# Agent attention and an ELU feed-forward layer on one core: half rounds of 512 query tokens with a tail of 192, one GpSimd pass of low parts a step, two of eight steps in float32

## The chip, the core and the metric

The kernel runs on one core of a Trainium2 chip. TensorE (PE) multiplies matrices; VectorE (DVE), ScalarE (ACT) and GpSimd (POOL) do the elementwise work; the SyncE queue (SP) issues the DMAs. The metric is the device time of one execution in microseconds, lower is better.

## The reference

Two batches of 12480 tokens with 128 channels go through attention by way of 49 agents, and the result through a feed-forward layer of width 2048 with ELU. Queries, keys and agents are drawn with a standard deviation of 0.8, so that the softmaxes are not flat.

```
def sm(a, b):
    s = scale * (a @ b.transpose(0, 2, 1))
    s = s - s.max(-1, keepdims=True)
    e = np.exp(s)
    return e / (e.sum(-1, keepdims=True) + 1e-09)
agent_v = sm(agents, k) @ v
x = sm(q, agents) @ agent_v                      # (2, 12480, 128)
h = x @ w_in                                      # 128 -> 2048
g = np.where(h > 0, h, np.exp(np.minimum(h, 0)) - 1)
out = g @ w_out                                   # 2048 -> 128
```

All inputs and the output are float32; the weights w_in and w_out are float64 and are converted on the chip.

## The kernel before

Since q2a @ agent_v @ w_in is associative, the kernel makes A = agent_v @ w_in once a batch (49 agents by 2048, `A_pe`, `A_out`) and never forms x. The probabilities of the queries, transposed to agents by tokens, are the moving operand of a first product with A, which gives h; the ELU of h is the moving operand of a second product with w_out.

*Tiles.* A round is G = 960 query tokens, 8 tiles (R) of 120 (TP), 13 rounds (NG) a batch, 26 in all. A tile's 120 tokens stand on partitions 0 to 59 and 64 to 123 (TQ = 124, HP = 60). A half round is T = 480 tokens, and a step is one half round with one of NP = 8 chunks of 256 hidden units: S = 416 steps. A step's tiles are 128 partitions by 2 x 480.

*A step.* `p1` (L418) multiplies: A and the probabilities are each split into a high part in float32r and the rest, also in float32r, and three products (high by high, high by low, low by high) are summed, each as a pair of matmuls on the upper and the lower half of the array's rows (`ROWS` = 0 and 64, tiles px and py, of which py is a copy of px with the halves exchanged, made by DMA, L355 and L356). `elu` takes exp(h - 1) on ACT (L424, bias from the tile `mone`) and min(e, 1) max h on DVE (L426), which is ELU + 1; the surplus is taken off at the end through the column sums of w_out (`w_sums`, `ncs`). `split` casts this g to a high part (float32r, ACT, L205) and subtracts it for the low part (`rest`, L210), in two passes of 480 columns: the first on POOL, the second on POOL or, in the chunks of `LO_DVE` = 0, 2 and 7, on DVE. `p2` (L456) sums low w by high g, high w by high g, high w by low g: six pairs of matmuls. In the one chunk of `PLAIN` = 3 there is no split; w and g are multiplied in float32, four matmuls, which the trace records as eight. After chunk 7 the two PSUM halves are joined: a DVE copy (L468), an ACT pass with `ncs` (L471), a POOL sum (L472) and the output DMA.

*Order.* The schedule is written by hand. The loop over steps at the end of the kernel issues in step s: `p1(s)`, `p2(s - 4)` (LAG), `elu(s)`, `split(s - 1)`, then what `at(s, ...)` has put there. A visit (`visit`, `plan`) is the attention work of one PSUM slot: scores of queries (L297) or of the second batch's keys (L166), or its sum of values (L225). After a query visit come, at fixed steps, the exponential, the sum (L317), the guard of 1e-9 and the reciprocal (`q_rz`: L322 and L325), the normalisation into `pp` (`q_mul`, L331), and the ring (`q_ring`): transposes on PE (L337), px on ACT and DVE, four DMAs to py. PSUM has three slots of two banks for h and visits (`ps_h`) and one bank each for the two output sums (`ps_o`).

*Prologue.* Scores of the first batch's keys (`sc`) alternate with the conversion of the weights (`conv`: `f64_steps`, L105 to L118, on DVE, ACT and POOL, with scratch tiles fr and ex in two buffers each; the product on POOL goes to `win_sb`, or for w_out to a passing tile "even", from which w_hi and w_lo are made); then come the exponentials, the sum over the values (L225), `w_sums` (L488) and A for the first batch.

Of the kernel before, what the change touches and what calls it, by code (L numbers as in the profile page):

```python
# [16 lines left out]
TP = 120  # L17
HP = TP // 2
TQ = 64 + HP
# [5 lines left out]
def tile_agent_attention_moe(  # L25
# [19 lines left out]
    T = G // 2  # L45
    NG = N // G
    NR = NG
    S = B * NG * NM
# [26 lines left out]
    w_f = big.tile([128, len(PLAIN), 2, 128], F32)  # L75
# [22 lines left out]
    def f64_steps(raw, out):  # L98
# [3 lines left out]
        fr = conv_pool[0].tile([128, n], I32, tag="fr", name="fr")  # L102
        ex = conv_pool[0].tile([128, n], I32, tag="ex", name="ex")
# [23 lines left out]

    def load_q(j):
        b, r = divmod(j, NG)
        t = kq_p.tile([C, G], F32, tag="q", name="q", bufs=2)  # L130
        nc.sync.dma_start(out=t, in_=qT[b, :, r * G:(r + 1) * G])
        q_t[j] = t
# [157 lines left out]
    def q_scores(j, ps):  # L290
        q_st[j] = {"ps": ps}
        src = q_t.pop(j)
        for t in range(R):
            for u in range(0, TQ, groups[0]):
                w = min(groups[0], TQ - u)
                x = t * TP + u - (64 - HP) * (u >= 64)
                nc.tensor.matmul(out=ps[u:u + w, t * NA:(t + 1) * NA], lhsT=src[:, x:x + w], rhs=ag_sb[:, j // NG, :], start=True, stop=True)  # L297

    def q_max(j):
        v = q_st[j]["ps"][:TQ, 0:R * NA].rearrange("p (t a) -> p t a", a=NA)  # L300
        mx = sm_p.tile([TQ, R], F32, tag="mx", name="mx")
        nc.vector.tensor_reduce(out=mx, in_=v, axis=AX.X, op=ALU.max)  # L302
        q_st[j]["mx"] = mx

    def q_sub(j):
        ps = q_st[j].pop("ps")
        v = ps[:TQ, 0:R * NA].rearrange("p (t a) -> p t a", a=NA)
        e = sm_p.tile([TQ, R, NA], F32, tag="qe", name="qe", bufs=2)
        nc.vector.tensor_tensor(out=e, in0=v, in1=q_st[j]["mx"].unsqueeze(2).to_broadcast([TQ, R, NA]), op=ALU.subtract)
# [17 lines left out]
    def q_mul(j):
        e = q_st[j]["e"].rearrange("p (h i) a -> p h i a", h=2)
        z = q_st[j]["z"].rearrange("p (h i) -> p h i", h=2).unsqueeze(3).to_broadcast([TQ, 2, R // 2, NA])
        out = pp.rearrange("p i (h a) -> p h i a", h=2)[:, :, :, 0:NA]  # L330
        nc.vector.tensor_tensor(out=out, in0=e, in1=z, op=ALU.mult)  # L331

    def q_tr(j, ps):
        for i in range(R // 2):
# [3 lines left out]
        q_st[j]["tr"] = ps[:NA2, :, 0:T // 2].rearrange("p u (i t) -> p u i t", t=HP)  # L338
# [4 lines left out]
    def q_parts(j, part):  # L343
# [3 lines left out]
        x = sm_p.tile([NA2, T], F32R, tag=f"px{part}", name=f"px{part}")  # L347
        y = sm_p.tile([NA2, T], F32R, tag=f"py{part}", name=f"py{part}")
# [6 lines left out]
        nc.sync.dma_start(out=y[a].bitcast(F32), in_=x[b].bitcast(F32))  # L355
# [448 lines left out]
```

## Time and profile before

| | us |
|---|---|
| median of 3 runs | 971.9 (971.7 to 974.7) |
| the profiled execution | 973.33 |
| its span, first to last instruction | 971.6 |
| PE busy | 949.6 (98%) |
| weight loads on PE busy | 796.2 (82%) |
| ACT busy | 847.6 (87%) |
| POOL busy | 833.8 (86%) |
| DVE busy | 807.5 (83%) |

The main loop of steps begins at about 58.6 us, with the first matmul of L418, and its last matmul starts at 966.9 us. The mean granted clock of TensorE is 0.994 of full speed. Durations in the rows are those of this one execution; a matmul's end is modelled, so the spacing of starts says more than a duration.

### The profile page before, as it was taken

Reading aid. Unit: us, or ns where it says so; the run is one execution under the profiler, and the core shown is the slowest. Engines: PE = TensorE matmul, PEld = TensorE weight load, DVE = VectorE, ACT = ScalarE, POOL = GpSimd, SP = SyncE. Lnnn points to the kernel's source line nnn. Section 1 sums busy time; section 2 is a strip of 40 time slices with the busy share of each in tenths; the row PEclk is TensorE's granted clock in tenths of the full one; section 3 lists DMA queues with packets and bytes.
Section 4 is the critical chain, followed back from the end, with each engine's and each line's share of the span. In section 5 each row is a group of like instructions: output and inputs, shape, how many; then the busy total and the mean of one; then the engine's idle time right before and its main releaser. Section 6 shows DMA issues by size and latency. Waiting matters only on the chain.

```text
span 971.6 us, 26490 instructions
## 1 busy us (share of the span) xinstructions
PE 949.6 (98%) x10894; PEld 796.2 (82%) x10894; DVE 807.5 (83%) x948; ACT 847.6 (87%) x967; POOL 833.8 (86%) x648
## 2 busy tenths in 40 slices
PE   7889999999999999999999999999999999999997
PEld 5777888888888888887888889788888888798886
DVE  7849788889888888788888889888988888898876
ACT  4648999988989889988998998989989989989996
POOL 3237888888988988988998998998989989989997
PEclk9989999999999999999999999999999999999999
DMA  9941232224232211012002101111020021001000
GB/s 349 398 141 53 99 94 78 68 74 119 68 93 79 68 32 58 28 42 68 27 26 64 37 27 52 38 39 59 20 79 27 22 68 38 27 12 37 28 21 21
DMA packets 26195, 67.47 MB, mean 69 GB/s; under 512 B 3239, under 2 KB 15171, under 8 KB 26075
## 3 DMA queue, kind: packets, MB, share of 16 engines
q1 hardware_dynamic: 26075, 65.79, 20.4%
q8 instruction: 85, 1.39, 0.6%
q14 instruction: 35, 0.29, 0.1%
HBM read 43.11 MB, written 12.78 MB: 58 GB/s over the span
## 4 chain that ended last, share of the span: by engine, by line
PE 79%; DVE 11%; issue 4%; ACT 3%; POOL 1%; DMA 1%; SPq 0%; POOLq 0%; DVEq 0%; ACTq 0%
PE o L456 49%; PE h L418 24%; DVE g L426 4%; PE h L225 3%; DVE lo L210 2%; ACT e L424 2%; POOL lo L210 1%; PE h L297 1%; PE h L166 1%; DVE ob L468 1%; DVE pp L331 1%; ACT hi L205 1%; DVE m_all L174 1%; DMA k<-in_kT_dram 1%; DVE mx L302 1%
## 5 line engine op out<-in xcount | busy, mean ns | idle before, releaser
L210 POOL TENSOR_TENSOR lo<-g,hi 128x480 fp32r<-128x480 f32 x571 | 744.3, 1339 | 96.6 <-ACT hi L205 37.4
L426 DVE SCALAR_TENSOR_TENSOR g<-e,h 128x960 f32<-128x960 f32 x416 | 474.2, 1148 | 101.6 <-ACT e L424 97.1
L424 ACT ACTIVATE e<-h,mone 128x960 f32<-128x960 f32 x416 | 440.9, 1061 | 40.9 <-PE h L418 31.7
L205 ACT ACTIVATE hi<-g 128x960 fp32r<-128x960 f32 x364 | 365.0, 1003 | 23.2 <-DVE g L426 22.7
L418 PE MATMUL h<-py,ahi 50*128 50x480 f32 x832 | 273.3, 408 | 1.1 <-DVE m_all L174 1.0
L418 PE MATMUL h<-px,ahi 50*128 50x480 f32 x832 | 273.7, 408 | 0.6 <-DVE g L426 0.4
L456 PE MATMUL o<-lo,w_hi 64*128 64x480 f32 x1456 | 224.5, 380 | 3.6 <-POOL lo L210 3.6
L456 PE MATMUL o<-hi,w_lo 64*128 64x480 f32 x1456 | 222.3, 378 | 1.6 <-ACT hi L205 1.3
L456 PE MATMUL o<-hi,w_hi 64*128 64x480 f32 x1456 | 221.3, 376 | 0.0
L418 PEld LDWEIGHTS h<-py,ahi 50*128 50x128 f32 x832 | 149.8, 186 | 22.4 <-issue 9.4
L418 PEld LDWEIGHTS h<-px,ahi 50*128 50x128 f32 x832 | 149.9, 186 | 20.9 <-issue 11.6
L210 DVE TENSOR_TENSOR lo<-g,hi 128x480 fp32r<-128x480 f32 x157 | 165.2, 1053 | 1.1 <-ACT hi L205 1.1
L456 PEld LDWEIGHTS o<-lo,w_hi 64*128 64x128 f32 x1456 | 141.5, 184 | 25.8 <-POOL lo L210 9.8
L456 PEld LDWEIGHTS o<-hi,w_lo 64*128 64x128 f32 x1456 | 143.9, 186 | 19.3 <-ACT hi L205 1.6
L418 PE MATMUL h<-px,alo 49*128 49x480 f32 x416 | 157.4, 378 | 0.0
L418 PE MATMUL h<-py,alo 49*128 49x480 f32 x416 | 157.3, 378 | 0.0
L456 PEld LDWEIGHTS o<-hi,w_hi 64*128 64x128 f32 x1456 | 142.8, 184 | 16.2
L456 PE MATMUL o<-g,w_f 64*128 64x480 f32 x416 | 92.6, 562 | 0.0
L418 PEld LDWEIGHTS h<-py,alo 49*128 49x128 f32 x416 | 77.9, 187 | 4.9
L418 PEld LDWEIGHTS h<-px,alo 49*128 49x128 f32 x416 | 78.1, 188 | 4.5 <-DVE alo L281 0.2
L472 POOL TENSOR_TENSOR ob<-ob,oa 128x480 f32<-128x480 f32 x51 | 76.3, 1496 | 0.0
L456 PEld LDWEIGHTS o<-g,w_f 64*128 64x128 f32 x416 | 40.6, 185 | 24.1 <-issue 21.6
(101 smaller groups left out, 544.6 us busy)
## 6 DMA issues: line engine op xcount, KB each, us to landing
k<-in_kT_dram SPq DMA_DIRECT2D x26, 480.0 KB
q<-in_qT_dram SPq DMA_DIRECT2D x26, 480.0 KB
out_dram<-ob SPq DMA_DIRECT2D x51, 240.0 KB
v<-in_vx_dram SPq DMA_DIRECT2D x13, 516.0 KB
v<-in_vx_dram SPq DMA_DIRECT2D x13, 483.8 KB
py<-px SPq DMA_DIRECT2D x52, 93.8 KB
py<-px SPq DMA_DIRECT2D x52, 91.9 KB
raw<-in_w_in_dram SPq DMA_DIRECT2D x4, 512.0 KB
```

What stands on the lines that cost most here:

```text
L166: nc.tensor.matmul(out=ps[u:u + w, j * NA:(j + 1) * NA], lhsT=src[:, x:x + w], rhs=ag_sb[:, b, :], start=True, stop=True)
L174: nc.vector.tensor_reduce(out=m_all[:, :, r], in_=view.rearrange("p (t a) -> p a t", a=NA), axis=AX.X, op=ALU.max)
L205: nc.scalar.activation(out=out, in_=x, func=ACTF.Copy)
L210: eng.tensor_tensor(out=out, in0=x, in1=hi.bitcast(F32), op=ALU.subtract)
L225: nc.tensor.matmul(out=ps[u:u + 64], lhsT=e[:, j * NA:j * NA + 64], rhs=v_t[b, r][:, j, :], start=(r == rs[0] and j < 2), stop=(r == rs[-1 ...
L297: nc.tensor.matmul(out=ps[u:u + w, t * NA:(t + 1) * NA], lhsT=src[:, x:x + w], rhs=ag_sb[:, j // NG, :], start=True, stop=True)
L302: nc.vector.tensor_reduce(out=mx, in_=v, axis=AX.X, op=ALU.max)
L418: nc.tensor.matmul(out=h[:, u, 0:T], lhsT=a[x, :], rhs=p[u ^ half][x, :], start=i == 0, stop=i == 2)
L424: nc.scalar.activation(out=e, in_=h, func=ACTF.Exp, bias=mone, scale=1.0)
L426: nc.vector.scalar_tensor_tensor(out=g, in0=e, scalar=1.0, in1=h, op0=ALU.min, op1=ALU.max)
L456: nc.tensor.matmul(out=o_t[u][:, 0:T], lhsT=w[x], rhs=v[x, :], start=first and i == 0, stop=last and i == len(jobs) - 1)
L472: nc.gpsimd.tensor_tensor(out=ob, in0=ob, in1=oa, op=ALU.add)
```

## The change

A round is now 1024 query tokens, 8 tiles of 128 (TQ = 128, HP = 64), a half round 512 (T). 12480 is 12 such rounds a batch and a tail of 192 tokens, which is a half round of its own with two tiles; the second tile's columns overlap the first so that both are full, and the first 64 columns are skipped. That makes 50 half rounds and S = 400 steps: 384 of 512 columns and 16 of 192. A round of keys stays at 960.

`PLAIN` is (3, 7): two of eight chunks are multiplied in float32 by `p2`; the steps of a tail all are, because `is_split` asks for a full width. The low parts of a split step are one POOL pass over 128 by 1024; `LO_DVE` is gone (DVE keeps the low part of px in the ring). All of w_out is kept in float32 (`w_f`), `w_sums` is taken from it, and the tile "even" goes; fr and ex have one buffer each.

The exponentials of the queries stand in two fixed tiles with a 50th column that holds 1e-9, and the sum runs over 50 columns, so that L322, the DVE operation that added the guard, goes. The bias of L424 is the constant -1.0 in place of a tile. The visits of queries keep their distance of 21 steps ahead of their round, now counted from `begin[j]`; the ring of the second batch's first round is put 7 steps ahead of it.

The diff, cut to its core:

```diff
-HP = TP // 2
-TQ = 64 + HP
+TQ = 128
+HP = TQ // 2
...
-    T = G // 2
-    NG = N // G
-    NR = NG
-    S = B * NG * NM
+    NR = N // G
+    T = TQ * R // 2
+    NF = N // (2 * T)
+    NG = NF + 1
+    TAIL = N - NF * 2 * T
+    NT = -(-TAIL // TQ)
+    SKIP = NT * TQ - TAIL
+    halves = [(b * NG + r, i) for b in range(B) for r in range(NG) for i in range(1 if r == NF else 2)]
...
+    S = len(halves) * NP
-    PLAIN = (3,)
+    PLAIN = (3, 7)
-    LO_DVE = (0, 2, 7)
...
-    w_f = big.tile([128, len(PLAIN), 2, 128], F32)
+    w_f = big.tile([128, NP, 2, 128], F32)
...
+    qe = [const.tile([TQ, R, NK], F32, name=f"qe{i}") for i in range(2)]
...
-        fr = conv_pool[0].tile([128, n], I32, tag="fr", name="fr")
-        ex = conv_pool[0].tile([128, n], I32, tag="ex", name="ex")
+        fr = conv_pool[0].tile([128, n], I32, tag="fr", name="fr", bufs=1)
+        ex = conv_pool[0].tile([128, n], I32, tag="ex", name="ex", bufs=1)
...
     def q_sum(j):
-        q_st[j]["z"] = sm_p.tile([TQ, R], F32, tag="z", name="z")
-        nc.vector.tensor_reduce(out=q_st[j]["z"], in_=q_st[j]["e"], axis=AX.X, op=ALU.add)
-    def q_rz(j, half):
-        if half == 0:
-            nc.vector.scalar_tensor_tensor(out=z, in0=z, scalar=1e-9, in1=z, op0=ALU.add, op1=ALU.max)
...
+        nc.vector.tensor_reduce(out=z, in_=q_st[j]["full"], axis=AX.X, op=ALU.add)
+    def q_rz(j):
+        nc.vector.reciprocal(out=z, in_=q_st[j]["z"])
...
     def is_split(s):
-        return at_step(s)[2] in SPLIT
+        return s % NP in SPLIT and width(s) == T
...
-        nc.scalar.activation(out=e, in_=h, func=ACTF.Exp, bias=mone, scale=1.0)
+        nc.scalar.activation(out=e, in_=h, func=ACTF.Exp, bias=-1.0, scale=1.0)
...
-        hi_t[s] = g_p.tile([128, 2, T], F32R, tag="hi", name="hi", bufs=4)
-        cast_hi(nc.scalar, hi_t[s], g_t[s])
-        lo_t[s] = []
-        for i in range(2):
-            eng = nc.vector if s == S - 1 or i and s % NP in LO_DVE else nc.gpsimd
-            lo_t[s].append(g_p.tile([128, T], F32R, tag=f"lo{i}", name=f"lo{i}", bufs=3))
-            rest(eng, lo_t[s][i], g_t[s][:, i, :], hi_t[s][:, i, :])
+        hi_t[s] = hi = g_p.tile([128, 2, T], F32R, tag="hi", name="hi", bufs=4)
+        cast_hi(nc.scalar, hi, g)
+        lo_t[s] = lo = g_p.tile([128, 2, T], F32R, tag="lo", name="lo", bufs=3)
+        rest(nc.gpsimd, lo, g, hi)
...
+        begin = [halves.index((j, 0)) * NP for j in range(B * NG)]
         for j in range(12, B * NG, 2):
-            plan(NM * (j - 2) + 11, f"q{j} q{j + 1}")
+            plan(begin[j] - 21, f"q{j} q{j + 1}")
...
+            if j % NG == 0:
+                ring = begin[j] - 7
```

## Rows read from the trace of the kernel before

**Rows 1.** page, part 1: busy us (share of the span) xinstructions, by engine

```profile
PE 949.6 (98%) x10894; PEld 796.2 (82%) x10894; DVE 807.5 (83%) x948; ACT 847.6 (87%) x967; POOL 833.8 (86%) x648
```

**Rows 2.** the waits, 93 to 960 us: who waited for whom: us, times, longest

```profile
DVE g L426 <- ACT e L424: 92.4, 137, 1.2
PEld o L456 <- POOL lo L210: 6.6, 14, 0.7
PE o L456 <- POOL lo L210: 1.7, 7, 0.3
```

**Rows 3.** the chain of waits in order of time: start us, us, what

```profile
45.22 2.91 PE h L488 x24
501.93 2.62 PE o L456 x24
506.59 0.22 PE h L337 x7
558.20 1.61 PE o L456 x8
567.70 1.31 PE h L418 x12
651.38 1.52 PE h L297 x128
718.71 1.52 PE h L297 x128
```

**Rows 4.** groups: line engine op out<-in xcount | busy us, mean ns | idle

```profile
L456 PE MATMUL o<-g,w_f 64*128 64x480 f32 x416 | 92.6, 562 | 0.0
```

**Rows 5.** one window (length, then busy us by engine, PEclk, DMA), and timeline within

```profile
64.80:68.10 3.30, 3.03 (x15) 2.50 (x16) 1.49 (x3) 1.42 (x2) 3.14 (x3) 0.50 0.00 0
65.75 1.40 PE L456 MATMUL o<-hi,w_hi 64*128 64x480 f32 x4
66.55 1.40 PE L456 MATMUL o<-lo,w_hi 64*128 64x480 f32 x4
```

**Rows 6.** groups of POOL and DVE passes, then three single ones from the timeline

```profile
L210 POOL TENSOR_TENSOR lo<-g,hi 128x480 fp32r<-128x480 f32 x571 | 744.3, 1339 | 96.6 <-ACT hi L205 37.4 <-issue 35.8 <-PE o L456 23.1
L210 DVE TENSOR_TENSOR lo<-g,hi 128x480 fp32r<-128x480 f32 x157 | 165.2, 1053 | 1.1 <-ACT hi L205 1.1
L472 POOL TENSOR_TENSOR ob<-ob,oa 128x480 f32<-128x480 f32 x51 | 76.3, 1496 | 0.0
L118 POOL TENSOR_TENSOR win_sb<-fr,ex 128x512 f32<-128x512 f32 x4 | 5.2, 1301 | 13.9 <-DVE fr L115 13.9
L118 POOL TENSOR_TENSOR even<-fr,ex 128x256 f32<-128x256 f32 x7 | 5.0, 727 | 20.6 <-DVE ncs L625 14.9 <-DVE fr L115 5.8
...
64.40 0.66 DVE L210 TENSOR_TENSOR lo<-g,hi 128x480 fp32r<-128x480 f32 x1
64.45 1.69 POOL L210 TENSOR_TENSOR lo<-g,hi 128x480 fp32r<-128x480 f32 x1 [11.94 <-ACT hi L205]
70.90 1.22 POOL L210 TENSOR_TENSOR lo<-g,hi 128x480 fp32r<-128x480 f32 x1 [2.22 <-ACT hi L205]
```

**Rows 7.** groups of the activation's DVE and ACT passes, the same columns

```profile
L426 DVE SCALAR_TENSOR_TENSOR g<-e,h 128x960 f32<-128x960 f32 x416 | 474.2, 1148 | 101.6 <-ACT e L424 97.1 <-POOL lo L210 2.7
L424 ACT ACTIVATE e<-h,mone 128x960 f32<-128x960 f32 x416 | 440.9, 1061 | 40.9 <-PE h L418 31.7 <-DVE g L426 6.3 <-ACT hi L205 0.3
L205 ACT ACTIVATE hi<-g 128x960 fp32r<-128x960 f32 x364 | 365.0, 1003 | 23.2 <-DVE g L426 22.7
```

**Rows 8.** timeline of the first conversions: start us, us, engine line op out<-in

```profile
7.98 0.42 DVE L105 TENSOR_SCALAR ex<-raw 128x512 int32<-128x512 int32 x1
8.15 1.39 POOL L118 TENSOR_TENSOR win_sb<-fr,ex 128x512 f32<-128x512 f32 x1 [6.38 <-DVE fr L115]
8.32 1.51 DVE L107 TENSOR_SCALAR fr<-raw 128x512 int32<-128x512 int32 x1
```

**Rows 9.** timeline near the end, in brackets the idle time before and its releaser

```profile
965.52 0.49 PE L456 MATMUL o<-lo,w_hi 64*128 64x480 f32 x2 [1.08 <-POOL lo L210]
```

More of the change, by code (lines that the diff above doesn't have):

```diff
@@ L126, in load_k, with tiles @@
         k_t[b, r] = t
+    def tiles(j):
+        return NT if j % NG == NF else R
     def load_q(j):
         b, r = divmod(j, NG)
[L130 to L131 removed]
+        n = tiles(j) * TQ
+        x = N - n if r == NF else r * 2 * T
+        t = kq_p.tile([C, 2 * T], F32, tag="q", name="q", bufs=2)
+        nc.sync.dma_start(out=t[:, 0:n], in_=qT[b, :, x:x + n])
         q_t[j] = t
@@ L305, in q_sub @@
     def q_sub(j):
[L306 to L309, printed above, removed]
+        n = tiles(j)
+        v = q_st[j].pop("ps")[:, 0:n * NA].rearrange("p (t a) -> p t a", a=NA)
+        q_st[j]["full"] = qe[j % 2][:, 0:n]
+        e = qe[j % 2][:, 0:n, 0:NA]
+        nc.vector.tensor_tensor(out=e, in0=v, in1=q_st[j]["mx"].unsqueeze(2).to_broadcast([TQ, n, NA]), op=ALU.subtract)
         q_st[j]["e"] = e
@@ L397, in wo_lo, with span, width @@
             if x in SPLIT:
-                rest(eng, w_part(w_lo, x), w_e.pop(x), w_part(w_hi, x))
+                rest(eng, w_part(w_lo, x), w_f[:, x].rearrange("p m d -> p (m d)"), w_part(w_hi, x))
     h_t, e_t, g_t, hi_t, lo_t, o_t = {}, {}, {}, {}, {}, {}
     def at_step(s):
-        x, c = divmod(s, NP)
-        return x // 2, x % 2, c
+        return (*halves[s // NP], s % NP)
+    def span(s):
+        j, half, c = at_step(s)
+        if j % NG == NF:
+            return slice(SKIP, SKIP + TAIL), N - TAIL
+        return slice(0, T), (j % NG) * 2 * T + half * T
+    def width(s):
+        x = span(s)[0]
+        return x.stop - x.start
     def is_split(s):
-        return at_step(s)[2] in SPLIT
+        return s % NP in SPLIT and width(s) == T
     def p1(s):
@@ L414, in p1 @@
         hi, lo = p_t[j]
+        n, y = width(s), span(s)[0]
         for i, (a, p) in enumerate([(ah, hi), (ah, lo), (al, hi)]):
@@ L455, in p2 @@
                 x = slice(r, r + 64)
-                nc.tensor.matmul(out=o_t[u][:, 0:T], lhsT=w[x], rhs=v[x, :], start=first and i == 0, stop=last and i == len(jobs) - 1)
+                nc.tensor.matmul(out=o_t[u][:, 0:m], lhsT=w[x], rhs=v[x, :], start=first and i == 0, stop=last and i == len(jobs) - 1)
         if last:
-            oa = o_p.tile([128, T], F32, tag="oa", name="oa")
-            ob = o_p.tile([128, T], F32, tag="ob", name="ob")
+            oa = o_p.tile([128, T], F32, tag="oa", name="oa")[:, 0:m]
+            ob = o_p.tile([128, T], F32, tag="ob", name="ob")[:, 0:m]
             pa, pb = o_t[0], o_t[1]
-            n = j * G + half * T
+            n = j // NG * N + span(s)[1]
             if s == S - 1:
-                for x in (slice(0, T // 2), slice(T // 2, T)):
+                for x in (slice(0, m // 2), slice(m // 2, m)):
                     nc.scalar.activation(out=oa[:, x], in_=pa[:, x], func=ACTF.Identity, bias=ncs[:, 0:1])
```

100 lines of the change are left out of this document (47 added, 53 removed).

## The prediction

> **What bounds the kernel now.** I read the busy shares first: TensorE (PE) stands at 98% of the span, ScalarE (ACT) and GpSimd (POOL) at 87% and 86%, VectorE (DVE) at 83% [rows 1]. A busy share alone proves little, since the ends of matmuls are modelled, so the waits came next: between 93 and 960 us the loads and matmuls of the second product waited 6.6 + 1.7 us for POOL's low parts [rows 2], and that is the largest wait of PE for another engine. Third, the chain of waits, merged in order of time: long unbroken pieces of PE, from which the spacing of its instructions comes. Matmuls run in pairs, one on each half of the array's rows. 24 of L456 take 2.62 us and 12 of L418 1.31 us, so a pair of 480 columns on split (float32r) operands takes 0.2183 us; the 8 records of a plain step's second product take 1.61 us [rows 3]. A split step is thus 9 pairs = 1.965 us, a plain step 3 pairs + 1.61 = 2.265 us. Two scores of queries take 1.52 us (128 records, 16 tiles), the transposes of a round 0.22 us [rows 3].
>
> As a test I add up one stretch: from the score visit at 651.38 to the next at 718.71 lie 32 steps, 67.33 us [rows 3]. 28 split steps are 55.0, 4 plain ones 9.1, the visit and two rounds of transposes 2.0: 66.0 us. So 1.3 us in 67.3 (1.9%) is not PE's own work. PE paces the loop, and a change is worth what it does to PE's work, plus at most the rest: 1.9% of the loop's some 908 us, 17 us.
>
> **The change, part by part.** All sums start from the profiled execution, 973.3 us; it lies 1.4 us above the median of 971.9, which I take off at the end.
>
> *Columns and plain steps on PE.* Before: 416 steps, 3 pairs of the first product in each (1248), 364 split steps with 6 more (2184): 3432 pairs x 0.2183 = 749.2 us, and 52 plain products x 1.61 = 83.7 [rows 3, 4]. Sum 832.9. After: 2 x 24 half rounds of 512 and 2 tails of 192, 8 steps each; 384 full steps, of them 288 split and 96 plain, and 16 narrow steps, all plain. 384 x 3 + 288 x 6 = 2880 pairs of 512 columns. No row shows 512, so I bound it. If the pair's time goes with columns it is 0.2183 x 512/480 = 0.2329; if only 480/2.4 = 200 ns of it does, 0.2133 + 0.0183 = 0.2316. I take 0.2329, for this reason: in the stretch with half the clock granted (0.50), a second product starts 0.80 us after another of two pairs, 0.40 a pair, which is 480 columns at 1.2 GHz with nothing on top [rows 5]; a fixed cost should have shown there. 2880 x 0.2329 = 670.7 (667.0 at the other bound). The 96 plain products take 1.61 x 512/480 = 1.717 each, 164.9. Tails: a narrow pair lies between a bare weight load, 2.91 us for 24 = 0.121 us, and a full pair, 0.2183 [rows 3]; I take 0.121 since 192 columns stream in less: 48 x 0.121 = 5.8 (10.5 at most). Their plain products: 16 x 1.61 x 192/480 = 10.3. Sum after: 851.7. **Term: +18.8 us** (15.1 to 23.5). Most of it is the second plain step: 1.717 against 6 x 0.2329 = 1.397 for a split one, 0.32 us x 48 half rounds = 15.4.
>
> The Trainium skill, "TensorE: Matmul & The Clock Gate", section Back-to-back issue gap, gives columns/2.4 + 2.5 ns: 202.5 ns for 480 and 215.8 for 512. The rows do not agree for split operands (218.3), so the measurement decides; worked through with the page's figures the two sums would differ by +23.7 instead of +18.8.
>
> *Scores and transposes.* 13 x 8 x 2 = 208 tiles of queries become 196: 12 x 1.52/16 = 1.1 us less, transposes some 0.2 less. **Term: -1.3.** The loads of queries, the score visits and the copies of the probabilities keep their lead over the round that uses them; a load grows from 480 to 512 KB, and the SP queue has fewer output DMAs in all.
>
> *Low parts on POOL alone.* DVE gives up 157 passes of 1.053 us, POOL's 571 passes of 480 become 288 of 1024. What does one cost? A POOL pass of 480 took 1.22 us with DVE idle of such work (at 70.90) and 1.69 us while DVE ran its own low part (64.40 and 64.45); the mean of 1.339 mixes both [rows 6]. 256 columns of another two-input pass took 0.727, 512 took 1.301: 2.24 ns a column. So 1.22 + 544 x 2.24 = 2.44 us alone; the upper bound is 1.339 x 1024/480 = 2.86. I take 2.44, since DVE no longer runs low parts. A half round then needs 6 x 2.44 + 1.5 (the output sum) = 16.1 us of POOL. PE needs 6 x 9 x 0.2329 + 2 x (3 x 0.2329 + 1.717) + 0.5 of scores and transposes = 17.9. POOL stays under PE: cost nil. The wait for a low part now covers both halves, but a split lands a step after its activation and is used some three steps later; POOL's idle share is the cover, and if it goes, POOL paces (rival C).
>
> *DVE and ACT.* DVE per half round: 8 x 1.148 x 512/480 = 9.8 plus round work of under 3, against 17.9. ACT: 8 x 1.061 and 6 x 1.003, scaled by 512/480, 15.5 plus about 1.3 [rows 7]. Both stay under PE, so the guard in the 50th column (one DVE operation fewer a round) and the constant bias are worth nothing of themselves. What DVE's relief can give back is PE's waits: of the 8.3 us on POOL [rows 2] I count 4, and 1 in the ramp after 60 us where DVE shares in everything. **Term: -5** (0 to -17, all that the stretch left over).
>
> *Prologue.* The converter's two scratch tiles become single. At the start the second weight conversion (DVE, 7.98) begins before POOL has read the first one's tiles (8.15 + 1.39 = 9.54) [rows 8]; it would have to wait 1.6 us, with the score reductions queued behind it on DVE and then the scores on PE behind those. In return DVE's L107, which took 1.51 us beside POOL where its neighbour took 0.42, runs free. **Term: +1** (-0.5 to +2.7).
>
> *The first tail, amid the program.* After 8 narrow steps the full ones come back: for four steps PE has a first product of 0.70 and a narrow second one of 0.64, 1.35 us, while ACT needs 2.2 a step. At most 4 x 0.85 = 3.4 us; three PSUM slots cover part. **Term: +1.5** (0 to 3.4). The ring of the round after it is put 7 steps ahead; two of these still hold full second products, so some 8 us remain for its copies.
>
> *The end.* The last steps are narrow and need no low part, so the stall of 1.08 us on POOL goes [rows 9], and the join of the output covers 192 columns instead of 480. **Term: -1.8.**
>
> Sum: 973.3 + 18.8 - 1.3 - 5 + 1 + 1.5 - 1.8 = 986.5; less 1.4 is **985 us**.
>
> **The rivals.** *A, faster: 512 columns cost PE no more than 480.* If the spacing of a split pair were set by something other than columns (its weight loads, say), the pair would stay at 0.2183, 2880 x 0.0146 = 42 us would go, and the time would be 943. It decides from 0.228 us a pair (13 us / 2880 less than 0.2329). For it: 0.2183 is 18 ns more than 480 columns at 2.4 GHz need, and nothing in the rows explains these. Against it: the 0.40 us at half clock is exactly columns [rows 5]. Chance 0.10. Beside it, the page's 215.8 ns for 512 columns would be such an outcome; no run here shows that width.
>
> *B, no change: the idle share is vector work's doing.* If all 17 us that PE's own work leaves open go, rather than 5, the time is 973. For it: POOL and ACT at 86% and more, and DVE waiting 92.4 us for ACT [rows 2]. Against it: what the waits name is 8.3 us. The Trainium skill, "Perfetto Trace Analysis", section Identifying the Most-Contended Engine, speaks for it: it calls matmul busy time a poor measure and would read the loads' 82% [rows 1], which leaves PE a margin; the spacing in [rows 3] does not agree. Chance 0.10, of which a third ends faster.
>
> *C, slower still: POOL paces.* At 2.86 us a pass a half round is 6 x 2.86 + 1.5 = 18.7 us of POOL, 0.8 over PE, 48 x 0.8 = 38 us: 1023. It decides above (17.9 - 1.5)/6 = 2.73 us a pass. Against it: 1.22 alone at 480. Chance 0.05.
>
> **How the numbers follow.** The forecast has the remaining 0.75. Its own bounds: PE's term alone spans 15.1 to 23.5, the stalls 0 to -17, prologue and tail together 5; taken together about 974 to 996. The range leaves A's centre and C outside (0.15) and holds B's slow side: 972 to 996. A measurement of this kernel can tell about 0.3% from no change. Faster by more than that, below 969: A and a third of B, 0.13. Within it, 969 to 974.8: the rest of B and the forecast's own edge, 0.10. Slower: 0.77.
>
> **What would show it.** In the profile after: 12 records of L418's line, or of a split step's second product, take 6 x 0.2329 = 1.40 us in the chain; 8 records of a plain product 1.72; 32 full steps between two score visits some 72.4 us; POOL's pass 2.4 to 2.5 us; DVE below 75%, PE still at 98%; a narrow step about 1.0 us. The forecast is wrong if split pairs of 512 columns come in under 0.228 us (A), if PE's left-over share falls from 1.9% to almost nothing (B), or if L456 waits for POOL for more than 20 us in total (C).

## The result, and the profile after

The changed kernel takes 986.75 us (median of 4 runs, 986.0 to 987.5), the kernel before it, timed beside it on the same chip, 971.8 us: 1.0148 times as long [1.0126, 1.017], some 15 us more. 985 was predicted. The profiled execution took 987.4 us, its span 985.6, 14.0 more than before. In the changed kernel L436 is the first product (before L418), L474 the second (L456), L443 the exponential (L424), L445 the ELU (L426), L213 the high part (L205), L218 the low part (L210), L304 the scores of queries (L297) and L340 the normalisation (L331).

Part 1 of the page, busy time (share of the span) and instructions of each engine, as [rows 1]:

```profile
PE 966.2 (98%) x10262; PEld 726.2 (74%) x10262; DVE 646.3 (66%) x747; ACT 765.9 (78%) x872; POOL 770.6 (78%) x362
```

VectorE, ScalarE and GpSimd all fell by 8 to 17 points and TensorE did not move. The waits from 93 to 960 us (who waited for whom: us, times, longest), as [rows 2]:

```profile
DVE g L445 <- ACT e L443: 202.8, 258, 1.5
POOL lo L218 <- ACT hi L213: 102.7, 83, 8.4
ACT e L443 <- PE h L436: 100.3, 159, 2.0
...
PEld o L474 <- POOL lo L218: 0.8, 1, 0.8
...
PE o L474 <- POOL lo L218: 0.4, 1, 0.4
```

PE's waits for low parts, 6.6 + 1.7 us before, are 0.8 + 0.4, all of it in one place, behind the first tail. The other engines now wait for PE or for one another. In the chain of waits (start us, us, what) PE holds 94%, before 79%:

```profile
111.13 1.72 PE o L474 x8
114.24 2.81 PE o L474 x24
...
541.02 0.69 PE h L436 x6
541.71 0.65 PE o L474 x8
...
599.38 1.52 PE h L304 x128
671.42 1.52 PE h L304 x128
```

24 records of split second products take 2.81 us, a pair of 512 columns thus 0.2342; elsewhere 12 take 1.40 or 1.41, 0.2333 to 0.235. I go on with 0.2335 (0.2329 was predicted). Eight records of a plain product take 1.72, of a narrow one 0.65, as forecast (1.72, 0.64). From one score visit to the next with 32 full steps between lie 72.04 us (forecast some 72.4; 67.33 before). PE's own work in them: 24 split steps of 9 x 0.2335 are 50.4, 8 plain ones of 3 x 0.2335 + 1.72 are 19.4, visit and transposes 2.0, in all 71.8. So 0.2 to 0.3 us of the stretch is not PE's own work, where before it was 1.3. The groups (line engine op out<-in xcount | busy us, mean ns | idle before, and its releaser), as [rows 6] and [rows 7]:

```profile
L218 POOL TENSOR_TENSOR lo<-g,hi 128x1024 fp32r<-128x1024 f32 x288 | 687.4, 2407 | 157.7 <-ACT hi L213 123.3 <-PE h L436 31.7 <-POOL lo L218 1.5
L445 DVE SCALAR_TENSOR_TENSOR g<-e,h 128x1024 f32<-128x1024 f32 x384 | 465.5, 1218 | 213.6 <-ACT e L443 211.6 <-POOL lo L218 0.4
L443 ACT ACTIVATE e<-h 128x1024 f32<-128x1024 f32 x384 | 391.9, 1025 | 114.8 <-PE h L436 101.9 <-DVE g L445 2.1 <-ACT hi L213 0.3
```

POOL's pass of 1024 takes 2.407 us, forecast 2.44.

**Where the 14 us lie.** I take the starts of the exponentials (timeline, L424 and L443) as marks. Behind the first tail the marks of the changed kernel mislead, since a narrow first product is short and its exponential starts early; so the figures with * are from the run e10 below, which is the changed kernel without that tail (10.0 is what it starts earlier by, from there on). Of before, 12288 tokens are 12.8 rounds, the last 0.8 taken as that share of a round; single marks scatter by about 1 us, read at the nearest marks batch 1 would be 426.5 and the line below it 1.3 longer. The last two lines are good to that only, their sum is not in question.

| stretch | before | after | more | by the prediction's terms |
|---|---|---|---|---|
| up to the first exponential | 59.6 | 62.1 to 62.4 | +2.5 | +1.0 |
| batch 0, 12288 tokens | 461.5 | 466.5* | +5.0 | +4.6 |
| batch 0, its last 192 tokens | 6.9 | 10.0* | +3.1 | +3.2 |
| batch 1, 12288 tokens | 427.8 | 429.5* | +1.7 | +4.6 |
| its last 192, to the end of the span | 15.8 | 17.5 | +1.7 | -0.1 |
| sum | | | +14.0 | +13.3 |

The last column is worked out from the prediction: the term of PE is 15.5 for the full steps and 1.65 for each tail, the scores' -1.3 and the relief's -5 go to the two halves of the full steps, stall and end to the tails. The sum was near; the relief on the full steps, the prologue and the end were not, in opposite directions. The experiments are about these, about the second plain chunk, and about what the prediction put at nothing.

### The profile page after: what moved, and what is told of

Same layout as the page of the kernel before. It is cut to its first block, busy times and chain, and to the rows that moved or that the text cites. A ratio compares the mean times of both kernels' runs of the same rounds, so it can differ in the third digit from the quotient of the medians.

```text
span 985.6 us, 24311 instructions
## 1 busy us (share of the span) xinstructions
PE 966.2 (98%) x10262; PEld 726.2 (74%) x10262; DVE 646.3 (66%) x747; ACT 765.9 (78%) x872; POOL 770.6 (78%) x362
## 4 chain that ended last, share of the span: by engine, by line
PE 94%; DVE 2%; POOL 1%; ACT 1%; DMA 1%; issue 0%; SPq 0%; DVEq 0%; ACTq 0%
PE o L474 58%; PE h L436 28%; PE h L233 3%; PE h L304 2%; PE h L174 1%; DMA k<-in_kT_dram 1%; PE h L349 1%; POOL lo L218 0%; DVE ex L116 0%; PE h L500 0%; DVE fr L118 0%; POOL w_f L121 0%; ACT ex L112 0%; DVE ex L108 0%; PE h L271 0%
## 5 line engine op out<-in xcount | busy, mean ns | idle before, releaser
L218 POOL TENSOR_TENSOR lo<-g,hi 128x1024 fp32r<-128x1024 f32 x288 | 687.4, 2407 | 157.7 <-ACT hi L213 123.3
L445 DVE SCALAR_TENSOR_TENSOR g<-e,h 128x1024 f32<-128x1024 f32 (+1 forms) x400 | 474.2, 1192 | 219.3 <-ACT e L443 217.2
L443 ACT ACTIVATE e<-h 128x1024 f32<-128x1024 f32 (+1 forms) x400 | 399.8, 1003 | 125.2 <-PE h L436 112.0
L213 ACT ACTIVATE hi<-g 128x1024 fp32r<-128x1024 f32 x288 | 303.1, 1053 | 11.6 <-DVE g L445 11.2
L436 PE MATMUL h<-px,ahi 50*128 50x512 f32 (+3 forms) x800 | 284.5, 435 | 0.8 <-DVE g L445 0.3
L436 PE MATMUL h<-py,ahi 50*128 50x512 f32 (+3 forms) x800 | 284.6, 435 | 0.0
L474 PE MATMUL o<-g,w_f 64*128 64x512 f32 (+1 forms) x896 | 193.7, 551 | 0.2 <-ACT oa L489 0.2
L474 PE MATMUL o<-hi,w_lo 64*128 64x512 f32 x1152 | 183.0, 394 | 1.4 <-ACT hi L213 1.4
L474 PE MATMUL o<-lo,w_hi 64*128 64x512 f32 x1152 | 181.9, 392 | 1.5 <-POOL lo L218 1.5
L474 PE MATMUL o<-hi,w_hi 64*128 64x512 f32 x1152 | 181.9, 392 | 0.0
L436 PEld LDWEIGHTS h<-px,ahi 50*128 50x128 f32 (+1 forms) x800 | 144.6, 187 | 35.1 <-issue 22.5
L436 PEld LDWEIGHTS h<-py,ahi 50*128 50x128 f32 (+1 forms) x800 | 144.5, 187 | 29.2 <-issue 9.9
L436 PE MATMUL h<-px,alo 49*128 49x512 f32 (+1 forms) x400 | 155.2, 388 | 0.0
L436 PE MATMUL h<-py,alo 49*128 49x512 f32 (+1 forms) x400 | 155.2, 388 | 0.0
L474 PEld LDWEIGHTS o<-lo,w_hi 64*128 64x128 f32 x1152 | 109.7, 186 | 27.6 <-POOL lo L218 2.4
L474 PEld LDWEIGHTS o<-hi,w_lo 64*128 64x128 f32 x1152 | 109.4, 186 | 26.1 <-ACT hi L213 1.5
L474 PEld LDWEIGHTS o<-hi,w_hi 64*128 64x128 f32 x1152 | 109.4, 185 | 25.4
L474 PEld LDWEIGHTS o<-g,w_f 64*128 64x128 f32 x896 | 84.4, 186 | 53.9 <-issue 45.4
L436 PEld LDWEIGHTS h<-px,alo 49*128 49x128 f32 x400 | 75.1, 188 | 8.1 <-DVE alo L289 0.2
L436 PEld LDWEIGHTS h<-py,alo 49*128 49x128 f32 x400 | 75.1, 188 | 8.0
L490 POOL TENSOR_TENSOR ob<-ob,oa 128x512 f32<-128x512 f32 (+1 forms) x49 | 69.5, 1418 | 11.4 <-ACT oa L489 11.3
```

Of the source, the lines that this page charges most:

```text
L213: nc.scalar.activation(out=out, in_=x, func=ACTF.Copy)
L218: eng.tensor_tensor(out=out, in0=x, in1=hi.bitcast(F32), op=ALU.subtract)
L436: nc.tensor.matmul(out=h[:, u, 0:n], lhsT=a[x, :], rhs=p[u ^ half][x, y], start=i == 0, stop=i == 2)
L443: nc.scalar.activation(out=e, in_=h, func=ACTF.Exp, bias=-1.0, scale=1.0)
L445: nc.vector.scalar_tensor_tensor(out=g, in0=e, scalar=1.0, in1=h, op0=ALU.min, op1=ALU.max)
L474: nc.tensor.matmul(out=o_t[u][:, 0:m], lhsT=w[x], rhs=v[x, :], start=first and i == 0, stop=last and i == len(jobs) - 1)
```

## The experiments

Ratios are to the kernel before on the same chip, with their 95% interval. "Before +" and "after +" name the kernel that was edited.

**What does the second plain chunk cost?** Before +, by itself (e6):

```diff
-    PLAIN = (3,)
+    PLAIN = (3, 7)
```

> The kernel before with two plain chunks (3 and 7) and nothing else: the low parts stay in two passes, on VectorE in the chunks 0 and 2 that are still split. Theory P: TensorE has 52 x (1.61 - 1.31) = 15.6 us more; GpSimd has 52 x 1.3 us less to do and VectorE 52 x 1.05, so some 3 us of waits go: +12 to +15 us against the kernel before, ratio 1.012 to 1.016. With the run at 480 that had the single pass as well (ratio 1.0076) this prices the single pass by itself: it would then be a gain of 5 to 8 us. Rival: the plain chunk costs only +7 us here too (ratio 1.007 to 1.009), and the single pass is worth nothing.

Measured: 981.7 us, ratio 1.0072 [1.0046, 1.0097], +7 us. By PE's work alone it should be 52 x (1.61 - 6 x 0.2183) = 15.6. The chain shows where the rest went:

```profile
591.86 1.52 PE h L297 x128
659.54 1.52 PE h L297 x128
727.20 1.52 PE h L297 x128
```

32 steps take 67.7 us. The ledger of PE's work is 24 x 1.965 + 8 x 2.265 + 2.0 = 67.3, so 0.4 is left over, not 1.3. The plain chunk makes no high and low parts, and with less vector work the stretch gives back 0.9 us. 15.6 - 7 = 8.6 us of relief in all, with some 2.5 either way by the interval: the rival of the expectation came out, and at this width the prediction's 5 was too small.

The same, with the low parts of the six split chunks in one GpSimd pass of 128 by 960 (e3):

```diff
-    PLAIN = (3,)
+    PLAIN = (3, 7)
...
-            rest(eng, lo_t[s][i], g_t[s][:, i, :], hi_t[s][:, i, :])
+        rest(nc.gpsimd, lo, g_t[s], hi_t[s])
```

> The kernel before with the other half of the change alone: two plain chunks (3 and 7) and one GpSimd pass of 128 x 960 for the low parts of a step, half rounds of 480 as they were. Theory P: TensorE has 52 x (1.61 - 1.31) = 15.6 us more, and about 4 us of waits for low parts go: 971.8 + 15.6 - 4 = 983 us (981 to 988). Rival: relieving VectorE and GpSimd gives back most of it: 972 to 976 us. The low pass of 960 columns takes 1.22 + 480 x 2.24 ns = 2.30 us by P.

Measured: 982.2 us, 1.0076 [1.0048, 1.0105], the pass 2269 ns. It can't be told from the run without the single pass. Once the stretch leaves only 0.4 us, taking DVE out of the low parts gives nothing more; the time that was expected came out, the split of it between the two edits did not.

**The changed kernel with one plain chunk (e2).** After +, and the low parts as before, two passes of 512 with the second on VectorE in chunks 0, 2 and 7 (in this and the next four runs of the changed kernel with one plain chunk or none, the running maximum `mrun` has one buffer, for room):

```diff
-    PLAIN = (3, 7)
+    PLAIN = (3,)
...
-        rest(nc.gpsimd, lo, g, hi)
+        for i in range(2):
+            rest(nc.vector if i and s % NP in (0, 2, 7) else nc.gpsimd, lo[:, i, :], g[:, i, :], hi[:, i, :])
```

> The changed kernel with one plain chunk and the low parts as before the change: two passes of 512 columns, in chunks 0, 2 and 7 the second of them on VectorE. What is left of the change is the width of 512, the tails, the guard column, the constant bias and the single scratch buffers. (The same small tile has one buffer.) Theory P: 986.75 - 15.4 = 971.4, plus about 4 us of waits for low parts that come back = 975 us (972 to 978). Rival: the width itself gains, because a longer matmul hides more: below 968 us. Rival: the width itself costs (tails, prologue, slower columns): above 980 us, so that the second plain chunk would explain less than half of the loss.

Measured: 975.3 us, 1.0010 [0.9996, 1.0023], as expected. Half rounds of 512 with their tails, and the rest of the change without the second plain chunk and the single pass, are together worth nothing. 1.0148 - 1.0010 is 1.38%, 13.4 us with some 2.5 either way, for these two. By PE's work alone the second plain chunk is 48 x (1.72 - 6 x 0.2335) = 15.3 us, so at 512 columns they gave back only some 2, where e6 gave back 8.6 at 480. Two score visits of this run, with 64 steps between them:

```profile
592.15 1.52 PE h L304 x128
...
734.99 1.52 PE h L304 x128
```

That is 71.4 us for 32 steps. PE's own work in them is 28 x 2.1015 + 4 x 2.42 + 2.0 = 70.5, so 0.9 is left over, where the kernel before has 1.3 in 67.3: a part of the relief came with the wider steps already, which are fewer and so have fewer passes.

A better share of the low parts (e7): one pass a step, on GpSimd but for chunk 7, which VectorE takes, and the scratch tiles of the conversion with two buffers again (raw with three in place of four, for room, and one load of weights moved behind two of keys):

```diff
-    PLAIN = (3, 7)
+    PLAIN = (3,)
...
-        rest(nc.gpsimd, lo, g, hi)
+        rest(nc.vector if s % NP == 7 else nc.gpsimd, lo, g, hi)
```

> A version meant to beat both: the changed kernel with one plain chunk, the low part of chunk 7 in one pass on VectorE and the other six on GpSimd, two buffers for the scratch tiles of the weight conversion (room from three instead of four load buffers for raw weights, the fourth weight load issued after the key loads). Theory P with S: TensorE 17.7 us a half round, GpSimd 6 x 2.38 + 1.4 = 15.7, so that it keeps its gaps and nothing starves: 986.75 - 15.4 - 1 = 970 us, ratio to the kernel before 0.995 to 1.000, no half clock after 80 us. Rival: VectorE's pass of 1024 columns starves behind GpSimd's: above 980 us.

Measured: 973.1 us, 0.9988 [0.9974, 1.0002]: at the slow edge of what was expected, not a measurable gain over the kernel before. Its score visits lie 70.9 us apart; PE's own work is the same 70.5.

All eight chunks split (e8), chunks 3 and 7 on VectorE (scratch single, raw and loads as in the run before):

```diff
-    PLAIN = (3, 7)
+    PLAIN = ()
...
+        rest(nc.vector if s % NP in (3, 7) else nc.gpsimd, lo, g, hi)
```

> No plain chunk at all in the full half rounds of 512: all eight chunks are split, the low parts of chunks 3 and 7 in one pass on VectorE, the others on GpSimd (raw weights in three load buffers). Theory P: TensorE 48 x 2 x 0.32 = 31 us less than in the changed kernel, 17.4 us a half round; GpSimd 15.7, ScalarE 8 x 0.95 + 8 x 0.95 + 1.3 = 16.5, VectorE 8 x 1.22 + 2 x 1.2 + 2.5 = 14.7, all below it: 956 to 962 us. Rival: with all engines over 90% the waits between them come back and one of the others paces: 970 us or more.

Measured: 1000.2 us, 1.0271 [1.0251, 1.0291]. PE's work goes down to 32 x 2.1015 + 2.0 = 69.2 a stretch, and the starts of the exponentials 32 steps apart lie 73.4 us apart in batch 1: 4.2 us are left over, and the expected 956 to 962 us are missed by some 40. So a plain chunk is not merely a loss of 0.32 us: it is also a step without two vector passes. The waits from 93 to 960 us and the group of VectorE's low parts:

```profile
PE h L436 <- DVE g L445: 24.9, 23, 1.4
...
PEld o L474 <- POOL lo L218: 6.4, 10, 0.8
...
L218 DVE TENSOR_TENSOR lo<-g,hi 128x1024 fp32r<-128x1024 f32 x96 | 175.2, 1825 | 2.4 <-ACT hi L213 1.2 <-issue 0.2
```

The first product waits for a PSUM slot, which the ELU frees, and the ELU shares VectorE with low parts of 1.8 us (1.43 in the run before). That the ELU stood behind them is read from these rows and was not tested, and the waits name only a part of what is left over. Which of the other pieces of that loop would have to shrink was not tried.

**All low parts on GpSimd, with seven split chunks (e1).** After +:

```diff
-    PLAIN = (3, 7)
+    PLAIN = (3,)
```

> The changed kernel with one plain chunk (3) in place of two (3 and 7); a half round then has seven low passes of 128 x 1024, all on GpSimd. (A small scratch tile has one buffer instead of two, to make room.) Theory P, the time is TensorE's own stream unless another engine needs more per half round: TensorE falls by 48 x 0.32 = 15.4 us, from about 18.0 to 17.7 us a half round, but GpSimd needs 7 x 2.36 to 2.41 + 1.42 = 17.9 to 18.3 us, so GpSimd paces: 987 - 15 + 48 x (0.2 to 0.6) = 981 to 1000 us, and the second product waits for low parts for over 20 us in total. Rival R, GpSimd has room enough: 971 us, and these waits stay at some 4 us. Rival Q, the plain step costs TensorE nothing that shows: 987 us with waits as in the changed kernel.

Measured: 1016.4 us, 1.0427 [1.0395, 1.046], slower than the changed kernel itself although PE has 15 us less to do. I had expected 981 to 1000 us, with more than 20 us of waits for low parts; those are 9.3 + 2.2. The largest wait of PE for another engine is another one. The waits from 93 to 960 us, the group of the normalisation (count: min/median/max ns), and the timeline at two of its places:

```profile
PE h L436 <- DVE g L445: 18.2, 6, 3.6
PEld o L474 <- POOL lo L218: 9.3, 16, 0.8
...
PE o L474 <- POOL lo L218: 2.2, 8, 0.4
...
L340 DVE TENSOR_TENSOR pp<-qe,qz x26: 562/1512/5868, 43.1 to 968.2; 128x392 f32<-128x392 f32 x24, 128x98 f32<-128x98 f32 x2
...
618.73 2.41 POOL L218 TENSOR_TENSOR lo<-g,hi 128x1024 fp32r<-128x1024 f32 x1
619.46 2.10 DVE L340 TENSOR_TENSOR pp<-qe,qz 128x392 f32<-128x392 f32 x1
...
652.27 4.82 POOL L218 TENSOR_TENSOR lo<-g,hi 128x1024 fp32r<-128x1024 f32 x2
657.00 1.33 POOL L490 TENSOR_TENSOR ob<-ob,oa 128x512 f32<-128x512 f32 x1
658.26 2.38 POOL L218 TENSOR_TENSOR lo<-g,hi 128x1024 fp32r<-128x1024 f32 x1
...
655.19 5.87 DVE L340 TENSOR_TENSOR pp<-qe,qz 128x392 f32<-128x392 f32 x1
662.28 1.02 ACT L443 ACTIVATE e<-h 128x1024 f32<-128x1024 f32 x1 [5.18 <-DVE g L445]
662.34 0.76 PE L436 MATMUL h<-px,ahi 50*128 50x512 f32 x1 [3.61 <-DVE g L445]
```

A VectorE operation of two SBUF operands that takes 0.56 us at its shortest lasts 5.87, until just after POOL's unbroken run ends at 660.64; behind it stand the ELU, the exponential and the first product. Six of the 26 last so long, 5.5 to 5.9 us, once in 32 steps from 577 us on, and each ends 0.4 us after POOL's run. All but the very first of the others end 0.4 us after the one pass that ran when they began, also where POOL goes on without a gap, as at 619.46. Why only some of them wait out three passes is not shown. Two windows behind one another show what came of that (length, busy us by engine, PEclk):

```profile
655.00:661.00 6.00, 3.73 (x32) 2.65 (x30) 6.00 (x3) 2.10 (x3) 5.64 (x3) 1.00 0.12 44
661.20:668.00 6.80, 5.66 (x32) 4.85 (x34) 4.92 (x5) 4.54 (x5) 3.46 (x2) 0.50 0.00 0
```

PE stood for more than a third of the first window, and in the second the granted clock is 0.50, 1.2 in place of 2.4 GHz. The Trainium skill, "GPSIMD Engine Reference", section Key points, says that GpSimd shares its SBUF interfaces with VectorE and that they contend where a VectorE instruction has two SBUF inputs. The trace agrees as to which operation suffers. To test it, the same kernel without L340 for rounds from the third on, so that this normalisation, a part of the computation, is left out (e5):

```diff
-                mid[s0 + NP] = [(q_mul, j)]
+                pass
```

> The kernel with one plain chunk and seven GpSimd passes a half round, once more, with one more part left out: the normalisation of the queries' probabilities (VectorE, product of two SBUF operands, L340) for every round but the first two, so that the output is not the reference's. In the run with that operation it lasted up to 5.87 us where its usual time is 0.34 to 0.64, while GpSimd ran passes one after another; the activation on VectorE, ScalarE and TensorE came to a stand behind it (3.6 us without a matmul), and the granted clock then fell to half for 6.8 us. Theory S, this starvation is what costs: without it GpSimd only paces, 7 x 2.38 + 1.4 = 18.0 us a half round as in the changed kernel, 985 to 995 us, and no half clock in the second half of the program. Rival G, GpSimd's load itself costs: the time stays above 1008 us.

Measured: 982.4 us, 1.0086 [1.0068, 1.0105], a little under the 985 to 995 expected. One DVE operation of half a microsecond at its shortest, left out 24 times, was worth 34 us; the stretch between score visits falls from 78.4 to 72.1. What is left, 72.1 us between score visits against 70.5 of PE's work, is GpSimd as the pace: by the starts of e1's timeline a pass takes 2.37 us and an output sum 1.26, seven and one are 17.9 us a half round, 71.4 in four. So the prediction's rival C had the right place and was one pass a half round away: six passes leave POOL its gaps, and in the changed kernel L340 lasts 0.64 us at the median and 1.06 at most.

**The prologue.** Before +, the scratch tiles single, as in the change (e4):

```diff
-        fr = conv_pool[0].tile([128, n], I32, tag="fr", name="fr")
-        ex = conv_pool[0].tile([128, n], I32, tag="ex", name="ex")
+        fr = conv_pool[0].tile([128, n], I32, tag="fr", name="fr", bufs=1)
+        ex = conv_pool[0].tile([128, n], I32, tag="ex", name="ex", bufs=1)
```

> The kernel before with one buffer each for the two scratch tiles of the weight conversion, nothing else. The first matmul of the main loop started at 58.6 us before and at 61.3 in the changed kernel. Theory P: the single buffers delay the conversions and with them the key scores, so this kernel's loop starts 1.0 to 2.7 us later, 973 to 974.5 us. Rival: the delay in the changed kernel comes from elsewhere (the position of the half clock, the longer weight work), and the single buffers cost nothing: 971.8 us, loop start at 58.6 +- 0.3.

Measured: 974.5 us, 1.0008 [0.9998, 1.0019], some 0.8 us longer and at most 1.9. In its trace the loop's first matmul starts at 61.35 us (before 58.6, changed kernel 61.34), 2.75 us later. Not all of that is shown to be the edit's. The last long piece of the chain ahead of the loop is the second part of the sum over the values. Here it is, with a window within it (length, busy us of PE, PEld, DVE, ACT, POOL, PEclk), in the kernel before, in this run and in e6, where the scratch tiles have two buffers:

```profile
48.13 7.82 PE h L225 x111
50.50:53.90 3.40, 3.40 (x60) 3.40 (x59) 0.00 (x0) 0.81 (x2) 2.01 (x3) 0.91 0.91 298
...
49.62 9.09 PE h L225 x112
50.50:53.90 3.40, 3.40 (x34) 3.40 (x32) 1.27 (x3) 1.23 (x3) 2.05 (x3) 0.50 0.54 122
...
48.43 9.35 PE h L225 x112
50.50:53.90 3.40, 3.40 (x36) 3.40 (x34) 0.00 (x0) 0.42 (x1) 1.64 (x3) 0.50 0.84 271
```

It starts 1.5 us later, which fits the conversions, and takes 1.3 us more at half the granted clock, 1.2 in place of 2.4 GHz; the latter e6 shows without the edit. The loop of e6 starts at 60.4 us, those of e3, e11 and e12, also with two buffers, at 61.1, 60.0 and 59.1. So single executions scatter by about as much as is to be explained, and the price of the edit is known only from the run's whole time.

**What sets the time of a pair?** After +, blocks of matmuls behind the last step that wait for nothing (e9; of the added lines, the pairs):

```diff
+        for n in (512, 480, 384, 256, 192, 128):
+            for i in range(16):
+                for u, r in enumerate(ROWS):
+                    nc.tensor.matmul(out=t[:, u, 0:n], lhsT=w_hi[r:r + 64, 2, i % 2], rhs=mv[r:r + 64, 0:n], start=True, stop=True)
...
```

> Adds to the changed kernel, behind its last step, blocks of matmuls with nothing to wait for: 16 split (float32r) row pairs each of 512, 480, 384, 256, 192 and 128 columns, 16 full-array ones of 512 and 256, then 8 plain (float32) row pairs of 512 and of 192. What sets the spacing of a split pair? Theory columns (the prediction's bound that was taken): time goes with columns, 0.455 ns each, so 0.233, 0.218, 0.175, 0.117, 0.087, 0.058 us. Theory fixed part: columns/2.4 plus 18 ns, so 0.231, 0.218, 0.178, 0.125, 0.098, 0.071. Rival load floor: the narrow ones stay at the 0.121 us that bare pairs of weight loads took, which is what the prediction assumed for 192 columns. The total gets longer by the added block, some 35 to 50 us, and is not compared.

Windows of these lines alone (length, PE busy, loads busy, PEclk), each from the first start of a width to the first of the next, 16 pairs (the last window, 128 columns, to its last start, 15 pairs and a bit):

```profile
980.72:984.48 3.76, 3.76 (x32) 3.53 (x34) 1.00 0.10 26
984.48:987.95 3.47, 3.47 (x35) 3.47 (x32) 1.00 0.00 0
987.95:990.75 2.80, 2.80 (x35) 2.80 (x33) 1.00 0.00 0
990.75:992.65 1.90, 1.90 (x35) 1.90 (x34) 1.00 0.03 9
992.65:994.42 1.77, 1.77 (x36) 1.77 (x34) 1.00 0.00 0
994.42:996.10 1.68, 1.68 (x35) 1.68 (x33) 1.00 0.00 0
```

A sixteenth of each: 512 columns 0.235 (its first pair, which follows other work, is slower), 480 0.217, 384 0.175, 256 0.119, 192 0.111; 128 take 0.11 too. From 256 to 480 columns the time goes with the columns, 0.45 to 0.46 ns each: columns alone forecast 0.175 and 0.117 for 384 and 256, a fixed part 0.178 and 0.125; so the fixed part of 18 ns is out, a few ns are not. Below that is a floor of 0.11, near the 0.121 of bare weight loads that the prediction took for 192 columns. A full-array float32r matmul of 512 takes 0.227 by its starts, no more than a pair of half-array ones.

**The first tail.** After +, its half round left out, with its two tiles of queries; those 192 tokens are not computed (e10):

```diff
-    halves = [(b * NG + r, i) for b in range(B) for r in range(NG) for i in range(1 if r == NF else 2)]
+    halves = [(b * NG + r, i) for b in range(B) for r in range(NG) for i in range(b if r == NF else 2)]
```

> The changed kernel with the first batch's tail left out: its 8 narrow steps, its 2 tiles of queries, its output (those 192 tokens are not computed). What did the tail amid the program cost? By the prediction's terms: 8 steps of 0.36 + 0.64 = 8.1 us, 0.2 of scores, 1.5 of stall: 9.8, so 977. By the times at which the exponentials start, batch 0's tail took 14.1 us: if all of that was the tail's own, 972.6. If the stall behind the tail is repaid later (three slots and a lead of four steps), less than 9.8: above 977.5.

Measured: 976.7 us, 1.0032 [1.0022, 1.0043]; 1.0148 - 1.0032 is 1.16%, 11.3 us, with some 2.4 either way. In the two traces the exponentials of the 8th, 16th, 24th and 32nd step of batch 1 lie 10.0 us apart. 9.8 was forecast; the 14.1 that the marks of the changed kernel suggested are not the tail's. The stall in it, read on PE's timeline by the gaps of starts: 0.45 us at 537.42, where a first product waits until VectorE has read the scores of the next rounds, 0.45 at 546.06 behind the ELU, 0.54 at 552.06 behind a low part; 1.44 together, 1.5 forecast.

**Nothing but the constant bias** (e11), and then, with it, one low pass a step (e12). Before +:

```diff
-        nc.scalar.activation(out=e, in_=h, func=ACTF.Exp, bias=mone, scale=1.0)
+        nc.scalar.activation(out=e, in_=h, func=ACTF.Exp, bias=-1.0, scale=1.0)
```

> The kernel before with the constant -1.0 as the bias of the exponential in place of the tile, nothing else. Prediction's step: ScalarE is under TensorE, worth nothing, ratio 0.999 to 1.001. Rival: the exponential gets about 0.09 us shorter (1025 ns at 1024 columns after against 1061 at 960 before), it stands in the loop from first product over exponential and ELU to the second product, and VectorE waited 92.4 us for it; some of the idle 1.2 us in 67.3 goes, 13 times: up to 15 us, ratio 0.985 to 0.997. The exponential should take about 0.97 us in both cases.

Measured: 974.1 us, 0.9993 [0.9982, 1.0005]. The exponential takes 970 ns in place of 1061, and that is worth nothing, as forecast: 67.2 us between score visits. The Trainium skill, "ScalarE: Activation LUTs", section What ACT_TABLE_LOAD costs, gives about 93 ns for each operand of an activation that is a pointer; the 91 here agree.

Then the low parts in one pass, on GpSimd in six chunks and on VectorE in chunk 7:

```diff
-            rest(eng, lo_t[s][i], g_t[s][:, i, :], hi_t[s][:, i, :])
+        rest(nc.vector if s == S - 1 or s % NP == 7 else nc.gpsimd, lo, g_t[s], hi_t[s])
```

> As the run with the constant bias at 480 columns, and the low parts of a split step in one pass of 128 by 960: on GpSimd in six of the seven split chunks, on VectorE in chunk 7 (before: two passes of 480, the second one on VectorE in chunks 0, 2 and 7). One plain chunk as before, no tails. If what was left over in the loop (1.2 us in 67.3) is the wait for low parts, the loop goes to some 66.6 a stretch and the time to 960 to 967; if it is nothing that elementwise work sets, 971 to 975.

Measured: 967.6 us, 0.9928 [0.9914, 0.9941], 0.7% faster than the kernel before and so faster than both, at the slow edge of the 960 to 967 expected. The chain, and the groups of low parts:

```profile
649.22 1.52 PE h L297 x128
715.66 1.52 PE h L297 x128
...
L210 POOL TENSOR_TENSOR lo<-g,hi 128x960 fp32r<-128x960 f32 x312 | 704.8, 2278 | 133.8 <-PE h L418 70.5 <-ACT hi L205 55.0 <-PE h L225 5.4
L210 DVE TENSOR_TENSOR lo<-g,hi 128x960 fp32r<-128x960 f32 x52 | 71.6, 1377 | 1.2 <-ACT hi L205 1.1
```

66.4 us a stretch, 0.3 to 0.4 over PE's own 66.0. VectorE does a third of its passes' number, in 71.6 us instead of 165.2, and GpSimd is done in 704.8 instead of 744.3 [rows 6]. Here nothing is paid for the relief on PE.

## Why the prediction was right, and where its terms were off

**PE paces, and its columns are the price: held.** The pair came out at 0.2335 and 0.2329 was forecast; 0.0006 on 2880 pairs is 1.7 us. The argument that chose columns over a fixed part, a second product of 0.80 us at half clock [rows 5], is borne out in the main by the widths of e9. Rival A falls with it: 512 columns are not free.

**The second plain step as most of the term: held.** It was put at 15.4 of the 18.8 us. e2 takes it out again, and the single pass with it, and stands at 1.0010; with the pair as measured it is 15.3 us of PE's work.

**GpSimd stays under PE: held**, at 2.407 us a pass for 2.44, with 0.8 + 0.4 us of waits. The cover that the prediction named is real and short: e1 uses it up. What it did not foresee is how that shows, by starving VectorE and not by waits for low parts; its sign of failure, waits of L474 for POOL of more than 20 us, would have missed it.

**DVE's relief, -5: too small.** This is the step that came out wrong, by size. The prediction counted half of the 8.3 us of waits with an engine's name on them [rows 2] and 1 us of ramp, and left the other 9 of the 17 us to nobody. On the full steps the time grew by 5.0 + 1.7 = 6.7 us. PE's work there grew by 15.5, 1.7 more with the pair as measured, less 1.2 of scores: 16.0. So some 9 us came back. That is rival B's mechanism, to a bit over half: in the second batch the idle share of a stretch went from 1.9% to under 0.5%, which the prediction had named as the sign of B. What B had wrong is that all of it would go and that nothing else would rise. Which edit gave the 9 us back is shown only in part: at 480 columns the plain chunk alone gives back 8.6 (e6), at 512 it and the single pass some 2 (e2), so the wider steps have a good share in it. The prediction has no term for these, and no run has the width alone.

**Prologue, +1: not settled.** In the profiled execution the loop begins 2.75 us later, and up to the first exponential 2.5 us are gone. But e4, with the same delay in its trace, is only 0.8 us longer (-0.2 to 1.9), and a part of the delay is the granted clock's, which e6 shows without the single buffers. In the two profiled executions the clock differs once more, behind the loop's start. Windows of the changed kernel and of the kernel before (length, busy us of PE, PEld, DVE, ACT, POOL, PEclk):

```profile
65.50:68.90 3.40, 1.73 (x12) 1.21 (x12) 2.56 (x4) 2.70 (x3) 1.57 (x1) 1.00 0.00 0
68.90:75.70 6.80, 5.94 (x142) 4.76 (x144) 1.81 (x3) 2.68 (x4) 4.42 (x3) 0.50 0.13 20
```

```profile
61.40:64.80 3.40, 2.06 (x17) 1.43 (x13) 3.36 (x5) 2.49 (x3) 0.35 (x1) 1.00 0.00 0
64.80:68.20 3.40, 3.13 (x17) 2.54 (x17) 1.49 (x3) 1.42 (x2) 3.24 (x3) 0.50 0.00 0
```

After a stretch in which PE was busy for 1.73 of 3.40 us (2.06 before), half the clock is granted for 6.8 us where it was 3.4 before; 3.4 us more at half speed are at most 1.7 us. That this is the change's doing is not shown: in the 17 executions of the kernel before that were timed beside e9 to e12, the mean granted clock runs from 0.988 to 0.994 and the time from 971.0 to 975.2 us. That batch 0 gave back less than batch 1 (some 3 us against 6) fits this in its sign, but no run separates it from the visits of keys and values, which only batch 0 has.

**First tail, +3.2: held**, its narrow steps, its stall and all (e10). **The end, -0.1: +1.7.** The stall on POOL did go, and behind the last matmul the span is 0.6 us shorter (4.0 against 4.6). Against that, as far as the 1 us of scatter lets it be told, from 960 to 982 us the gaps on PE's timeline add up to some 1.1 us, where the steps turn narrow (0.38 at 967.59) and where the last round's outputs are taken (0.38 at 974.84, 0.35 at 975.75), as much as went. No run takes the last tail out, so the rest of this line stays open.

So 985 was near 986.75 with the mechanism right, but that the sum came so close is luck in part: by the profiled executions the relief was some 4 us too small and, against it, a pair, a prologue and an end together were put some 5 us too low.

## What to carry to other kernels

Add up the pacing engine's own work over one period of the loop. What is left over is what elementwise work can give back at most, whether or not a wait has a name. Here edits that lightened VectorE or GpSimd took it from 1.3 us in 67 to 0.2 to 0.4, and over the whole run some 9 of 17 us came back, more than the waits named. Then look for the edit that lightens them without lengthening the pacing engine: at 480 columns a plain product that saves two vector passes gave back 8.6 us and cost 15.6, while relief from fewer and longer passes cost PE nothing and made the only faster kernel.

Before an engine is given all passes of one kind, add up its time per period too, and ask who shares its memory access: here the fault appeared at a short operation of another engine.

## What the runs showed of the hardware that was not expected

A VectorE operation with two SBUF operands can wait out several GpSimd passes that follow each other without a gap: six of 26 took 5.5 to 5.9 us, where the median is 0.64 us in the changed kernel and 1.1 in the kernel before, and leaving 24 of them out was worth 34 us of 1016. Others, beside the same unbroken run of passes, waited for one pass alone (2.10 us at 619.46). A subtraction of 128 by 960 in one VectorE pass takes 1.38 us, two of 480 took 2 x 1.05. And split pairs of half-array matmuls have a floor of 0.11 us at 192 columns and below, so that a narrow half round pays for columns that it does not have.
